# Zero products in PE's waits at the end of attention and in the first routing, a shorter list, and a later first step of the next routing

## The chip, the cores and the metric

One NeuronCore of a Trainium2 chip runs the whole program. Its engines work side by side: PE (TensorE) multiplies matrices, DVE (VectorE) and ACT (ScalarE) work on vectors, POOL (GpSimd) and SP (SyncE) mostly issue DMAs, POOL the ones that gather by an index. Each engine takes its instructions in the order in which the program wrote them and waits where an operand is not there. PE's clock has two levels, 1.2 and 2.4 GHz; the profile gives the granted clock of a stretch as a share of the higher one. The metric is the device time of one execution in microseconds (us); the time shown for a kernel is the median of its runs.

## What is computed

```python
scores = scale * np.matmul(q, k.transpose(0, 1, 3, 2))        # B, H, S, D = 4, 8, 576, 64
scores = np.where(masks[None], scores, -1e9)                  # a window, or a dilated window, by head
attn = np.exp(scores - max); attn /= attn.sum(-1) + 1e-9
x = np.matmul(attn, v)  ->  N = 2304 tokens of 512

logits = x @ w_gate                                           # E = 8 experts
for idx in np.argsort(-logits.flatten()):                     # greedy, largest logit first
    tok, e = idx // E, idx % E
    if assigned[tok] >= 0 or counts[e] >= N // E: continue    # cap = 288 tokens for each expert
    assigned[tok] = e; counts[e] += 1
x = for each e: relu(x[assigned == e] @ w1[e]) @ w2[e]        # F = 1024

P = exp(x @ w_gate2 - max), eight rounds of row and column scaling
out = sum over e of P[:, e] * (relu(x @ w1b[e]) @ w2b[e])     # every expert on every token
```

## The kernel before

**Attention** runs over NU = 25 units (a batch element, half of the heads, a block of rows). In the loop over n stand, for different units, the exponentials (ACT), the scores of the next unit (PE, L174 and L181), the transposes of the weights into the PSUM tile `ps_p` (`p_trans`, PE L207), their copy (`p_evac`, DVE or ACT), the product with V (`pv`, PE L228), the turn of its result (L270), and the logits of finished tokens (L300). Behind the loop stand the last turns and logits; a copy on DVE (L375) brings the logits to the router.

**The router** is written as a generator, `phase(ph)`, one phase for each expert. It finds the greedy choice not by sorting but expert by expert: the expert that fills up next is found by a search for its threshold, six steps (`STEPS`) of a few bits each. In a step DVE compares all tokens with the step's candidates (`G`, L504), PE counts with 18 small products (L576), DVE compares the counts with what is left (`ok`, L585), and PE adds up (`count`, L588), whose largest entry (`cur`, L590) starts the next step. Then comes the **list**: flags `ze`, two products with a matrix of ones and a triangular one (L618, L619), a scan and a few steps on DVE (L621 to L632) that give each token its place, two halves of a one-hot matrix (`G`, L640), 18 products (L671) that collect the token numbers, and `idx` (L676), by which POOL gathers the tokens (L877). `books()` (L654 to L660) brings mask and logits up to date, and a last product (L683) counts how much of each expert was used.

At each `yield` the generator hands out how much PE work, in ns, should lie between it and its next step. In phase 0 there is no such work; there `stage1` itself steps through it and puts two products of zeros (`warm(2)`, L808) where the number is over 2000. From phase 1 on `interleave` weaves the steps of the routing into the products of the expert found before:

```python
    room = 0.0
    for ns in main:
        room += ns
        while side is not None and room >= need:
            need = next(side, None)
```

`need` starts at 1900 and is then what the router hands out, times a factor.

**The first expert stage** (`main`) takes for each expert: the gathered tokens turned by PE (L922) and copied by ACT (`xt`, L923), the first layer (L907, ACT L912 and DVE L913 behind it), the second (L948), then the products of `m2_l1` and `m2_l2`, and `gate2` (L1283 to L1287), the logits of the second gate, whose last step is DVE's sum P (L1287). The weights w1a and w2a are gathered by POOL (L868) by the expert's number into four buffers `raw`, converted by ACT to a high half (L847) and by DVE to a low half (L838); `pump` calls these pieces at fixed places of the order, so DVE and ACT take them in the order of the program between the steps of the routing. The tiles `r` of the router have two PSUM buffers, shared with `gate2`.

**Stage 2** (L1176, L1214) runs every expert on every token and is the bulk of the time.

## Time and profile before

| | us |
|---|---|
| median of 3 runs | 1760.49 (1759.36 to 1765.73) |
| the profiled execution | 1749.37 |
| its span, first to last instruction | 1747.6 |
| PE busy | 1709.8 (98%) |
| DVE, ACT, POOL busy | 1341.5 (77%), 846.3 (48%), 238.6 (14%) |
| L1176 and L1214 in the chain that ended last | 27% and 25% |
| the routing of phase 0, from the first L576 to the first L907 | 111.87 to 145.08 |

PE is busy in 98% of the span. A busy PE is not a PE at its full clock: the granted clock is read for itself, by stretch. A row of a timeline gives the start, the duration, engine, line, operation, the tile written and those read, the count, and in brackets how long the engine was idle before and what released it. Durations of products contain a tail that overlaps the next one.

### The profile page before, as it was taken

Reading aid. Unit: us, or ns where it says so; the run is one execution under the profiler, and the core shown is the slowest. Engines: PE = TensorE matmul, PEld = TensorE weight load, DVE = VectorE, ACT = ScalarE, POOL = GpSimd, SP = SyncE. Lnnn points to the kernel's source line nnn. Section 1 sums busy time; section 2 is a strip of 40 time slices with the busy share of each in tenths; the row PEclk is TensorE's granted clock in tenths of the full one; section 3 lists DMA queues with packets and bytes.
Section 4 is the critical chain, followed back from the end, with each engine's and each line's share of the span. In section 5 each row is a group of like instructions: output and inputs, shape, how many; then the busy total and the mean of one; then the engine's idle time right before and its main releaser. Section 6 shows DMA issues by size and latency. Waiting matters only on the chain.

```text
span 1747.6 us, 34883 instructions
## 1 busy us (share of the span) xinstructions
PE 1709.8 (98%) x14326; PEld 1280.6 (73%) x14326; DVE 1341.5 (77%) x2572; ACT 846.3 (48%) x1544; POOL 238.6 (14%) x293
## 2 busy tenths in 40 slices
PE   9978999999999999999999999999999999999998
PEld 7956677767777577777777777777777777777777
DVE  6977777766647888878887887888788878886656
ACT  7833443334444455644445543565445544454433
POOL 1323333223410000000000000000000000000111
PEclk9977999999999999999999999999999999999999
DMA  9923444332733144343435235432544334433120
GB/s 330 279 59 110 124 125 134 95 98 77 213 99 102 76 163 154 137 159 112 176 127 209 88 138 211 155 130 89 201 161 157 123 131 155 165 138 148 37 100 37
DMA packets 107568, 241.19 MB, mean 138 GB/s; under 512 B 46384, under 2 KB 72496, under 8 KB 100496
## 3 DMA queue, kind: packets, MB, share of 16 engines
q1 hardware_dynamic: 86768, 151.64, 25.0%
q0 software_dynamic: 20384, 87.05, 14.3%
q8 instruction: 112, 1.84, 0.4%
q14 instruction: 48, 0.39, 0.1%
q10 hardware_dynamic: 256, 0.28, 0.1%
HBM read 173.64 MB, written 61.73 MB: 135 GB/s over the span
## 4 chain that ended last, share of the span: by engine, by line
PE 61%; issue 10%; DVE 5%; ACT 2%; POOL 1%; DMA 0%; POOLq 0%; ACTq 0%; DVEq 0%
PE mm L1176 27%; PE mm L1214 25%; PE mm L907 4%; PE mm L992 3%; PE mm L948 1%; DVE hl L1133 1%; POOL out_dram L1228 1%; ACT raw L1045 0%; DVE w1l L1048 0%; DVE r L1048 0%; DMA raw<-in_w2a_dram,widx 0%; DVE w2l L966 0%; PE r L576 0%; ACT hh L1132 0%; DVE xg L913 0%
## 5 line engine op out<-in xcount | busy, mean ns | idle before, releaser
L1176 PE MATMUL mm<-xb,w1h 128*128 128x384 f16 x2352 | 573.3, 326 | 1.3 <-DVE mm L1147 0.8
L1214 PE MATMUL mm<-w2h,hh 128*128 128x256 f16 x1764 | 480.8, 273 | 0.4 <-DVE t L1238 0.2
L1214 PE MATMUL mm<-w2l,hh 128*128 128x256 f16 x1764 | 480.8, 273 | 0.0
L1214 PE MATMUL mm<-w2h,hl 128*128 128x256 f16 x1764 | 480.8, 273 | 0.0
L1176 PE MATMUL mm<-xb,w1l 128*128 128x384 f16 x1176 | 383.3, 326 | 0.0
L1214 PEld LDWEIGHTS <-hh 128*128 128x128 f16 x3528 | 345.2, 98 | 43.0 <-issue 0.9
L1176 PEld LDWEIGHTS <-w1h 128*128 128x128 f16 x2352 | 230.0, 98 | 154.7 <-issue 6.6
L1214 PEld LDWEIGHTS <-hl 128*128 128x128 f16 x1764 | 172.6, 98 | 20.1
L1133 DVE TENSOR_TENSOR hl<-r,hh 128x1536 f16<-128x1536 f32 x84 | 147.5, 1756 | 41.2 <-ACT hh L1132 41.2
L1176 PEld LDWEIGHTS <-w1l 128*128 128x128 f16 x1176 | 115.0, 98 | 76.1
L1128 ACT ACTIVATE r<-mm 128x384 f32<-128x384 f32 x252 | 119.1, 481 | 100.5 <-PE mm L1176 100.5
L1094 POOL DMA_DIRECT2D ws<-raw x48 | 26.0, 541 | 928.6 <-ACT raw L1045 660.4
L1132 ACT ACTIVATE hh<-r 128x1536 f16<-128x1536 f32 x84 | 124.6, 1483 | 43.6 <-DVE r L1157 41.6
L1139 ACT ACTIVATE mm<-mm 128x384 f32<-128x384 f32 x84 | 40.3, 479 | 175.3 <-PE mm L1176 175.3
L1133 DVE TENSOR_TENSOR hl<-S,hh 128x1152 f16<-128x1152 f32 x84 | 113.5, 1351 | 0.0
L1224 DVE SCALAR_TENSOR_TENSOR acc<-t,P,acc 128x512 f32<-128x512 f32 x126 | 94.7, 752 | 4.5
L907 PE MATMUL mm<-xt,w1h 128*128 128x288 f16 x512 | 97.5, 290 | 0.0
L1132 ACT ACTIVATE hh<-S 128x1152 f16<-128x1152 f32 x84 | 96.4, 1147 | 0.4 <-DVE S L1161 0.4
L1045 ACT ACTIVATE raw<-raw 128x1024 f16<-128x1024 f32 x48 | 50.6, 1055 | 87.3 <-DVE raw L1029 45.8
L912 ACT ACTIVATE w1h<-mm 128x288 f16<-128x288 f32 (+1 forms) x120 | 46.9, 396 | 88.1 <-PE mm L907 87.9
L913 DVE SCALAR_TENSOR_TENSOR w1l<-mm,w1h 128x288 f16<-128x288 f32 (+1 forms) x120 | 50.0, 435 | 45.4 <-ACT w1h L912 45.3
L868 POOL DMA_INDIRECT raw<-in_w2a_dram,widx x64 | 75.9, 1186 | 55.3 <-issue 20.4
(265 smaller groups left out, 2921.5 us busy)
## 6 DMA issues: line engine op xcount, KB each, us to landing
xb<-xw SPq DMA_DIRECT2D x30, 1344.0 KB, 5.9
ws<-raw POOLq DMA_DIRECT2D x48, 448.0 KB, 3.3
ws<-r POOLq DMA_DIRECT2D x48, 448.0 KB, 3.0
raw<-in_w2b_dram SPq DMA_DIRECT2D x32, 512.0 KB, 4.4
raw<-in_w1b_dram SPq DMA_DIRECT2D x56, 256.0 KB, 9.0
w1h<-ws SPq DMA_DIRECT2D x6, 1792.0 KB
w1l<-ws SPq DMA_DIRECT2D x6, 1792.0 KB
w2h<-ws SPq DMA_DIRECT2D x6, 1792.0 KB, 7.2
```

What stands on the lines that cost most here:

```text
L868: self.nc.gpsimd.indirect_dma_start(out=r[:, i, :], out_offset=None, in_=rows[lay], in_offset=bass.IndirectOffsetOnAxis(ap=widx[:, c:c + 1 ...
L907: nc.tensor.matmul(p, a[:, k, 128 * f:128 * (f + 1)], rhs(k, b), start=(done[f] == 1 and i == 0), stop=(done[f] == KT and i == 2), skip_gr ...
L912: nc.scalar.activation(h[0][:, f, :n], p, AF.Relu)
L913: nc.vector.scalar_tensor_tensor(h[1][:, f, :n], p, 0.0, h[0][:, f, :n], op0=OP.max, op1=OP.subtract)
L992: nc.tensor.matmul(p, a[:, f, c], b[:, f, :], start=(f == 0 and n == 0), stop=(f == FT - 1 and n == 2))
L1045: self.nc.scalar.activation(hi[:, k], x, AF.Copy, scale=sw)
L1128: nc.scalar.activation(o, p, AF.Relu, scale=SH)
L1132: yield nc.scalar.activation(hq[0][:, i, k], x, AF.Copy)
L1133: yield V.tensor_sub(hq[1][:, i, k], x, hq[0][:, i, k])
L1176: nc.tensor.matmul(p, w[u][:, 2 * j + i // 2, k, 128 * (i % 2):128 * (i % 2 + 1)], x[:, v, r, j], start=(q in (1, 5) and j == 0 and n == 0 ...
L1214: nc.tensor.matmul(p, h[u][:, i, a, 128 * t:128 * (t + 1)], w[v][:, i, b, :], start=(q in (1, 7) and i == 0 and j == 0), stop=(q in (2, 3) ...
L1224: V.scalar_tensor_tensor(self.acc[:, r, :], x, self.P[:, r, e:e + 1], self.acc[:, r, :], op0=OP.mult, op1=OP.add)
```

## The change

It has six parts.

1. At the end of attention products of zeros are added on PE: `full` writes n of 128 columns to the unused end of a bank of the tile `ps_p` (12 ahead of the last scores but one, 18 between the last full unit's transposes and the next `pv`, 12 ahead of the turn of unit NU-2), and `busy` one of 512 columns behind each of the last logits and six at the end.
2. In phase 0 of the routing the zeros at each step are set by a table: 5 (for 2) ahead of each set of L576, 1 (for 0) ahead of each count, 6 (for 2) ahead of the list, 14 (for 2) ahead of L671; 24 (for 8) behind the list; and 2 behind the turns of each of the first two groups of tokens.
3. The list needs two steps less on DVE: the triangular matrix gets -1000 on its diagonal and the scan begins at 1000, so that a place of a token that isn't chosen is over 1000, and the smaller of two places replaces two products and a sum. `books` has one step more.
4. A small DMA `near` on POOL reads parts of the token array in phase 0 ahead of the gathers; the first gather then has fewer semaphores to wait for.
5. `interleave` begins with `need` 3300 for 1900. The first step that it places, the count of phase 1's first search step, then comes later among the first expert's products, and with it all steps behind it.
6. A second tile `z` of `ps_s` takes the zeros, and the last `ps_p` is allocated later.

```diff
+        def full(p, n):
+            for _ in range(n):
+                nc.tensor.matmul(p[:, 1, 4 * QB:], zero[:, :128], zero[:, :512 - 4 * QB], start=False, stop=False,
+                                 skip_group_check=True)
...
             if n < NU:
                 exps(n)
+            if n == NU - 3:
+                full(wide, 12)
             if n + 1 < NU:
                 scores(n + 1)
                 row_max(n + 1)
...
-                p_evac(n - 1, p_trans(n - 1))
+                wide = p_trans(n - 1)
+                if n == NU - 2:
+                    full(wide, 18)
+                p_evac(n - 1, wide)
...
-        last = [ps.tile([128, 2, 512], F32, name=name, bufs=1) for name in ("ps_v", "ps_p")]
+        last = [ps.tile([128, 2, 512], F32, name="ps_v", bufs=1)]
...
+        z = ps.tile([128, 2, 512], F32, name="ps_s")
+
+        def busy(n):
+            for _ in range(n):
+                nc.tensor.matmul(z[:, 0, :], zero[:, :128], zero, start=True, stop=True)
...
+        full(wide, 12)
         behind[-2]()
         x_turn(NU - 2, last[0])
         for n, c in enumerate(rest[:apart]):
             logits(o[:, n], c)
+            busy(1)
+        last.append(ps.tile([128, 2, 512], F32, name="ps_p", bufs=1))
         x_turn(NU - 1, last[1])
...
             logits(o[:, apart + n], c)
+            busy(1)
+        busy(6)
...
+FAR = 1000.0
...
-    f["tri"] = -(p[:, None] > p[None, :]).astype(np.float32)
+    f["tri"] = -(p[:, None] > p[None, :]).astype(np.float32) - FAR * np.eye(128, dtype=np.float32)
...
-        V.tensor_tensor_scan(out=pos, data0=self.one_f, data1=p[:, :2 * NC], initial=0.0, op0=OP.mult, op1=OP.add)
-        zv = wk.tile([128, 2 * NC], F32, name="zv")
+        V.tensor_tensor_scan(out=pos, data0=self.one_f, data1=p[:, :2 * NC], initial=FAR, op0=OP.mult, op1=OP.add)
         V.tensor_add(pos, pos, p[:, 64:64 + 2 * NC])
-        V.scalar_tensor_tensor(zv, pos, CAP + 0.5, ze, op0=OP.is_le, op1=OP.mult)
-        V.tensor_mul(pos, pos, zv)
         r = wk.tile([128, NC], F32, name="r")
-        V.tensor_add(r, pos[:, :NC], pos[:, NC:])
+        V.tensor_tensor(r, pos[:, :NC], pos[:, NC:], op=OP.min)
...
-            V.scalar_tensor_tensor(self.mask, zv[:, NC:], -100.0, self.mask, op0=OP.mult, op1=OP.add)
+            V.tensor_scalar(up, pos[:, NC:], CAP + 0.5, -100.0, op0=OP.is_le, op1=OP.mult)
+            V.tensor_add(self.mask, self.mask, up)
...
+IDLE = {4000: 5, 1900: 1, 2900: 5, 2400: 6, 6000: 14, 1200: 0}
...
+            if ph == 0 and g < 2:
+                self.warm(2)
             yield 640
...
-            if need > 2000:
-                self.warm(2)
+            self.warm(IDLE[need])
             if i in (2, 4):
                 late.pop(0)()
+            if i == 6:
+                near = self.xp.tile([38, 2], F16, name="near", bufs=1)
+                xd = self.xd
+                nc.gpsimd.dma_start(near, bass.AP(tensor=xd.tensor, offset=xd.offset + S * (B - 1) * 2 * DM,
+                                                  ap=[[30 * DM, 38], [DM, 2], [1, 1]]))
...
         next(first)
-        self.warm(8)
+        self.warm(24)
         next(side)
...
-        interleave(main(), side, lambda: SLACK if self.ph == 1 else SL2, need=1900)
+        interleave(main(), side, lambda: SLACK if self.ph == 1 else SL2, need=3300)
```

The order in PE's queue in one step of the first search (G the candidates' comparison, r the counts), before:

```order
L576 MATMUL r<-A,G 128x8
L588 LDWEIGHTS count
L588 MATMUL r<-ok,count 128x8
L808 LDWEIGHTS zero
L808 MATMUL mm<-zero 128x512
...
L576 LDWEIGHTS G
```

and in the changed kernel:

```order
L598 MATMUL r<-A,G 128x8
L831 LDWEIGHTS zero
L831 MATMUL mm<-zero 128x512
L610 LDWEIGHTS count
L610 MATMUL r<-ok,count 128x8
L831 LDWEIGHTS zero
L831 MATMUL mm<-zero 128x512
...
L598 LDWEIGHTS G
```

A zero product stands ahead of the count, and five instead of two behind it.

PE's queue where the first expert's first layer begins (xg gathered tokens, xt the turned ones), before:

```order
L922 LDWEIGHTS xg
L922 MATMUL mm<-id_102,xg 128x96
L588 LDWEIGHTS count
L588 MATMUL r<-ok,count 128x8
L808 LDWEIGHTS zero
L808 MATMUL mm<-zero 128x512
...
L907 LDWEIGHTS w1h
L907 MATMUL mm<-xt,w1h 128x288
```

and in the changed kernel:

```order
L945 LDWEIGHTS xg
L945 MATMUL mm<-id_102,xg 128x96
L831 LDWEIGHTS zero
L831 MATMUL mm<-zero 128x512
...
L930 LDWEIGHTS w1h
L930 MATMUL mm<-xt,w1h 128x288
```

The count of phase 1's first step has gone from here; it stands behind the first twelve products of the layer.

DVE's queue in the first layer (w2l the low half of a converted piece of w2a, w1l behind L913 that of the layer's result), before, from the second step's comparison on:

```order
L504 TENSOR_TENSOR G<-m,x 128x288 x2
L913 SCALAR_TENSOR_TENSOR w1l<-mm,w1h 128x288
L581 TENSOR_TENSOR base<-thr,x 128x32
L585 TENSOR_TENSOR ok<-r,rem 32x8
L838 SCALAR_TENSOR_TENSOR w2l<-raw,w2h 128x1024
L913 SCALAR_TENSOR_TENSOR w1l<-mm,w1h 128x288
L590 TENSOR_REDUCE cur<-r 128x1
...
L838 SCALAR_TENSOR_TENSOR w2l<-raw,w2h 128x1024
L581 TENSOR_TENSOR base<-thr,x 128x32
L585 TENSOR_TENSOR ok<-r,rem 32x8
L913 SCALAR_TENSOR_TENSOR w1l<-mm,w1h 128x288
L838 SCALAR_TENSOR_TENSOR w2l<-raw,w2h 128x1024 x2
```

and in the changed kernel:

```order
L526 TENSOR_TENSOR G<-m,x 128x288 x2
L936 SCALAR_TENSOR_TENSOR w1l<-mm,w1h 128x288
L861 SCALAR_TENSOR_TENSOR w2l<-raw,w2h 128x1024
L936 SCALAR_TENSOR_TENSOR w1l<-mm,w1h 128x288
L603 TENSOR_TENSOR base<-thr,x 128x32
L607 TENSOR_TENSOR ok<-r,rem 32x8
...
L861 SCALAR_TENSOR_TENSOR w2l<-raw,w2h 128x1024
L612 TENSOR_REDUCE cur<-r 128x1
...
L861 SCALAR_TENSOR_TENSOR w2l<-raw,w2h 128x1024 x2
L603 TENSOR_TENSOR base<-thr,x 128x32
L607 TENSOR_TENSOR ok<-r,rem 32x8
```

The second ok now stands behind the first w2l, the third behind all four.

## Rows read from the trace of the kernel before

**Rows 1.** The clock: mean granted TensorE clock and span of the core.

```profile
core 0: 1747.6 us, clock 0.988
```

**Rows 2.** By stretch: busy us of PE PEld DVE ACT POOL, PEclk, DMA.

```profile
108.40:116.40 8.00, 4.86 (x75) 3.02 (x72) 6.53 (x24) 0.83 (x3) 0.00 (x0) 0.50 0.09 25
...
143.80:149.40 5.60, 5.60 (x24) 3.19 (x24) 2.03 (x8) 1.47 (x2) 4.38 (x5) 0.51 0.54 150
149.40:161.60 12.20, 12.20 (x137) 9.39 (x136) 10.18 (x26) 5.53 (x9) 2.28 (x3) 1.00 0.31 86
```

**Rows 3.** PE's waits from 150 to 200 us: total, times, longest.

```profile
PE r L618 <- DVE ze L607: 1.2, 1, 1.2
PE r L576 <- DVE G L504: 1.0, 2, 0.7
PE r L671 <- DVE G L640: 0.6, 1, 0.6
PE mm L907 <- DVE x2l L953: 0.5, 1, 0.5
```

**Rows 4.** Line L683: PE idle before it, us and times, by releaser.

```profile
  DVE P L1287: 5.6, 5
```

**Rows 5.** PE's timeline, attention's end: start, duration, instruction [idle before, releaser].

```profile
93.05 0.38 PE L174 MATMUL ps_s<-mk 96*96 96x256 bf16 x2 [0.60 <-ACT e L200]
...
98.81 1.57 PE L228 MATMUL ps_v<-rawv,pt 128*96 128x65 f32 x16 [0.99 <-ACT x L244]
...
111.07 1.01 PE L808 MATMUL mm<-zero 128*128 128x512 f16 x2 [1.77 <-DVE L L375]
```

**Rows 6.** PE's timeline near the start: four zero products at full clock.

```profile
9.94 1.04 PE L161 MATMUL ps_v<-zero 128*128 128x512 f16 x4
```

**Rows 7.** PE's timeline, the search, and one set of L576 at full clock.

```profile
117.58 1.04 PE L576 MATMUL r<-A,G 128*128 128x8 f16 x18
118.86 0.16 PE L588 MATMUL r<-ok,count 32*128 32x8 bf16 x1 [0.24 <-DVE ok L585]
...
121.28 0.16 PE L588 MATMUL r<-ok,count 32*128 32x8 bf16 x1 [0.24 <-DVE ok L585]
...
149.36 0.77 PE L576 MATMUL r<-A,G 128*128 128x8 f16 x18
```

**Rows 8.** DVE's timeline, first list, and the third phase's chain to P.

```profile
129.24 0.20 DVE L624 SCALAR_TENSOR_TENSOR zv<-pos,ze 128x36 f32<-128x36 f32 x1
129.47 0.20 DVE L625 TENSOR_TENSOR pos<-pos,zv 128x36 f32<-128x36 f32 x1
...
221.49 0.17 DVE L590 TENSOR_REDUCE cur<-r 128x1 f32<-128x8 f32 x1 [2.17 <-PE r L588]
...
234.51 0.17 DVE L1287 TENSOR_TENSOR P<-r,P 128x16 f32<-128x16 f32 x1
```

**Rows 9.** PE's timeline, from the list to the first layer.

```profile
132.20 0.44 PE L671 MATMUL r<-rhs,G 128*128 128x6 f16 x9 [2.63 <-DVE rhs L647]
...
143.74 0.16 PE L588 MATMUL r<-ok,count 64*128 64x8 bf16 x1 [1.49 <-DVE ok L585]
...
145.08 0.69 PE L907 MATMUL mm<-xt,w1h 128*128 128x288 f16 x2
...
158.38 0.93 PE L576 MATMUL r<-A,G 128*128 128x8 f16 x18
```

**Rows 10.** ACT's timeline, conversions of weights and copies of xt.

```profile
139.21 1.06 ACT L847 ACTIVATE w1h<-raw 128x1024 f16<-128x1024 f32 x1 [1.30 <-DMA raw<-in_w1a_dram,widx]
140.64 2.46 ACT L923 ACTIVATE xt<-mm 128x768 f16<-128x768 f16 x3 [0.37 <-DMA oidx<-idx]
...
155.07 1.06 ACT L847 ACTIVATE w2h<-raw 128x1024 f16<-128x1024 f32 x1 [0.58 <-DMA raw<-in_w2a_dram,widx]
```

**Rows 11.** POOL's timeline, gathers of w2a, the first and the last.

```profile
140.48 1.70 POOL L868 DMA_INDIRECT raw<-in_w2a_dram,widx  x1 [2.21 <-DVE w1l L838]
...
151.28 1.01 POOL L868 DMA_INDIRECT raw<-in_w2a_dram,widx  x1 [0.30 <-issue]
```

More of the change, by code (lines that the diff above doesn't have):

```diff
@@ L804, in warm @@
     def warm(self, n, width=512):
+        if not n:
+            return
         p = self.psum()[:, :width]
@@ L1330, in stage1 @@
     def stage1(self, ctx, late):
+        nc = self.nc
         pool = lambda n, b: ctx.enter_context(self.tc.tile_pool(name=n, bufs=b, side="right"))
```

## The prediction

> **What bounds the kernel now.** I read the views in this order: the clock, the table by stretch, PE's waits, then the timelines of PE, DVE, ACT and POOL around the places that the diff touches. The profiled execution spans 1747.6 us [rows 1] and took 1749.4 us in all, so 1.8 us lie around the span; it is 11 us under the median of 1760.5. The sum below is made against 1749.4 and carried over to the median unchanged. A measurement of this kernel can tell about 0.5% from no change, 8.8 us; my chances go by that.
>
> PE is the bound nearly everywhere, and stage 2, over half of the time, is not touched. What the change can reach is small and lies in three places. First, the stretch from 108.4 to 149.4 us, in which PE ran at half clock (granted clock 0.50 and 0.51 of full, 1.2 GHz against 2.4) [rows 2]: the search for the first expert, its token list, the gathers and the entry to the first layer. Ahead of it PE had a few waits and tiny products; the clock came back after 5.6 us in which PE was busy without a gap, and stayed [rows 2]. Second, PE's 3.3 us of waits in the next phase [rows 3]. Third, five waits of 1.1 us, 5.6 us in all, before the product of L683, one in each later phase [rows 4]. Nothing else in PE's queue that the diff touches waits.
>
> **The end of attention.** Twelve zero products go ahead of the last scores but one, eighteen between the transposes of the weights and the product with V, twelve more ahead of the first of the last three turns. Four zeros of 512 columns took 1.04 us at full clock [rows 6], so one of 128 columns takes some 0.06. What the first twelve delay, 0.7 us, is taken up by the 0.60 us for which PE waited for ACT at 93.05; the third twelve and the products among the logits fall into waits that are there as well, and the last six into the 1.77 us before 111.07 [rows 5]. The eighteen, 1.1 us, have no cover: the product behind them feeds DVE, the next turn and ACT's copy, for which PE waits 0.99 us at 98.81 [rows 5], and so the end moves. I take **+1.05 us**; between +0.4 (if half is absorbed there) and +1.7 (both batches in full).
>
> Here a rule speaks against the change. The rows have a zero of 512 columns at 0.26 us with its tail, a quarter of which is what I use. The Trainium skill, "TensorE: Matmul & The Clock Gate", section "Back-to-back issue gap", says that in a real stream of a weight load and a product of 128 columns each pair takes about 81 ns, since the weight load is not hidden; every one of these zeros loads its weights anew. By that, an estimate from the page, the eighteen would cost 1.5 us and the sum would be 0.4 us worse. No run here shows such a stream, and the sum goes by the rows.
>
> **The search at full clock.** With zeros in all its waits PE is hardly idle from 105 us on, so I expect the clock to hold. One step takes 2.42 us from count to count; its 18 products take 1.04 us at half and 0.77 at full clock [rows 7], 0.27 less. The five zeros, 5 x 0.216 = 1.1 us, replace two at half clock, 1.04 us: no loss. The one more before the count lies in the wait for DVE's ok. Four or five of the six steps gain, one is bound by DVE: **-1.25 us** (0 to -1.6).
>
> **List and gathers.** DVE loses two of its steps between the scan and the index, one every 0.23 us [rows 8]: -0.46. The 14 zeros, 3.0 us, replace two at half clock and the wait of 2.63 us [rows 9], 3.65 together, less 0.46: covered. The products of L671 gain some 0.1 by the clock. **-0.6 us.** The small DMA `near` takes waits off the first gather of tokens; by the gap that it leaves that is worth 0 to 0.35 us on a path that does not bind here, so 0. Up to this point the index comes 0.8 us earlier.
>
> **The entry.** Before, the count of expert 1's first search step and three zeros stand ahead of the first layer, and PE waits 1.49 us for ok, which stands behind four conversions on DVE; the layer begins at 145.08 [rows 9]. Now twelve of its products stand ahead of that count. Next to bind is ACT: its fourth conversion of weights ends at 140.27, waiting for DMA, and three copies of xt take 2.46 [rows 10]; with 0.2 us less upstream the layer can begin at 142.7, 2.4 us earlier. Its first 18 products took 4.28 us at half clock (145.08 to 149.36) [rows 7, 9], half of that at full: 2.1 us more. So PE is 4.5 us ahead at 149.4.
>
> **Most of that is given back.** In the new DVE order the second ok stands behind the first w2l conversion and a w1l, and the third behind all four w2l; before, it stood ahead of the last two. These hang on the gathers of w2a: eight that start at 140.48, when DVE frees a buffer, run one after the other on POOL until 152.3 [rows 11], and ACT's last w2h waits for a DMA until 155.07 [rows 10]. They can come only about 0.6 us earlier (DVE's chain from the index, plus one more bookkeeping step, 0.2). PE reaches the second count at 148.5 and finds ok at 151.2: 2.8 us of waiting. It reaches the third at 155.7 and finds ok at about 157: 1.3 more. The same point of the layer lies at 157.65 in the trace of before (six products at 0.12 ahead of 158.38 [rows 9]). Left of 4.5: **-0.5 us** (this sum holds the three terms above and the +1.05). If the w2a gathers bind less, up to -4.5; if POOL comes no earlier, 0.
>
> **The later phases.** The other minimum, 3300 for 1900, puts the routing's steps 1.0 to 1.5 us of PE work later against the experts' products, in every phase. In the next phase the waits for ze, G and x2l, 3.3 us [rows 3], are reshuffled: PE asks later, and DVE has more behind it. The wait for ze should go, one of the others may grow: **-1.2 us** (+1 to -3.3). For L683 nine products of 256 columns more stand between the gate's products and it: 9 x 0.106 = 0.95 us (estimate from the products above). What it waits for is the end of a DVE chain that runs nearly without a gap from the last count at 221.49 to P's sum at 234.51 [rows 8]. That chain begins 1.1 to 1.4 us later, loses 0.46, gains 0.2, and some 0.5 of it now runs ahead of the count; so P comes 0.6 later and each wait shrinks by 0.4, five times: **-2.0 us** (0, if DVE moves as far as PE; -4.9, if DVE does not move). The bookkeeping's added step costs 0.2 us on DVE per phase; it is in this term.
>
> **Sum.** -0.5 - 1.2 - 2.0 = -3.7 us: 1745.7 by the profile, **1756.8** by the median.
>
> **The rivals.**
> - *The entry's gain is kept.* If the w2a pieces land 3 us earlier than I think, or ok(2) does not wait for them, the 4.5 us stay; with -2 in the next phase and -4 at L683 that is -10.5: 1750.0. For it: POOL's first gather took 1.70 us, the last 1.01 [rows 11], which could be contention that moves away. Against: the chain index, conversions, buffers, gathers is DVE's and POOL's, and the clock does nothing for these. Chance 0.22.
> - *New waits eat the rest.* The later steps of the routing meet other work on DVE; the waits at L683 stay at 1.1, those of the next phase stay at 3.3, and the entry gives back all. Then what is left is the cost of attention's zeros and one or two new waits of 0.5: +2, 1762.5. For it: the DVE chain ahead of L683 has hardly a gap [rows 8]. Chance 0.22.
> - *The clock falls all the same, and the zeros cost.* Place: from 108 to 143 us. A zero is 0.43 us at half clock; a step of the search is then 5 x 0.43 + 1.0 + 0.43 + 0.1 = 3.7 instead of 2.42 us, five times, +6; the 6 and the 14 ahead of list and gathers +3.2; the 24 run 10.3 us, longer than the tokens need, so that the first layer begins some 13 us late. It then runs at full clock and finds its weights, 2.3 back: +11, 1771.5. It decides only if half clock lasts through both search and list; if it lasts for a few microseconds, it is one step, +1. Against: 5.6 us without a gap brought the clock back [rows 2], and the stream of zeros has fewer gaps than that stretch's neighbours. Chance 0.06.
>
> **How the numbers follow.** Forecast 0.50, rivals 0.22, 0.22 and 0.06. The forecast's own bounds, entry 0 to -1.5, next phase +1 to -3.3, L683 0 to -4.9, make 1751 to 1762. The range leaves out the slow rival and the far half of the first: 1749 to 1766, its upper end being the second rival with another 3.5 us for the zeros of attention and a scatter of the median. Faster by over 0.5% (under 1751.7): most of the first rival, 0.22. Slower by over 0.5% (over 1769.3): 0.06. Within: 0.72.
>
> **What would show it.** Granted clock near 1.00 from 105 to 160 us; steps of 2.1 us in the search; the first layer beginning at about 142.7; PE waiting some 3 us for ok in its first third and then over 1 us more; waits at L683 (now at another line) of 0.6 to 0.8. Wrong, if PE does not wait there, if those waits stay at 1.1 or go altogether, or if half clock shows in the search.

## The result, and the profile after

The changed kernel took **1775.24 us** (median of six runs, 1773.53 to 1785.0) beside 1760.34 for the kernel before on the same chip: ratio **1.009, interval 1.0066 to 1.0114**, 15 us slower. The prediction was 1756.8 (1749 to 1766); it is wrong. The profiled execution took 1774.9 us.

The same kernel was measured three more times, each on another chip: 1.0017 [1.0003, 1.0032], 1.0021 [1.0012, 1.0031] and 1.0116 [1.0102, 1.0131]. So there are two things to explain: 3 to 4 us that are lost everywhere, where -3.7 was forecast, and 11 to 17 more that are lost on some chips.

Span and mean clock first (compare [rows 1]):

```profile
core 0: 1773.1 us, clock 0.989
```

Then the table by stretch (compare [rows 2]): time, length, busy time of PE, PEld, DVE, ACT and POOL with their counts, PE's clock, share of the DMAs, GB/s.

```profile
95.00:100.00 5.00, 5.00 (x74) 4.62 (x73) 3.55 (x7) 4.06 (x16) 2.44 (x4) 1.00 0.16 44
100.00:105.00 5.00, 3.70 (x38) 3.52 (x37) 1.99 (x5) 3.32 (x10) 2.98 (x4) 0.72 0.81 185
105.00:110.00 5.00, 5.00 (x53) 5.00 (x53) 1.59 (x5) 1.81 (x4) 2.33 (x4) 0.50 0.77 136
110.00:115.00 5.00, 5.00 (x55) 4.27 (x54) 3.52 (x13) 2.21 (x6) 0.38 (x1) 0.50 0.14 39
115.00:120.00 5.00, 5.00 (x80) 3.56 (x80) 2.63 (x10) 1.15 (x3) 0.00 (x0) 0.50 0.01 3
120.00:125.00 5.00, 4.93 (x32) 2.13 (x31) 1.84 (x8) 0.00 (x0) 0.00 (x0) 0.74 0.00 0
```

PE has no gap from 105 to 120 us, and yet runs at half clock there: the zeros fill its waits and the clock falls all the same. It fell at about 102 us, just behind a wait of PE for ACT, and came back between 122.5 and 123, behind the last zeros. Waits of PE from 95 to 200 us (us in total, times, longest):

```profile
PE r L610 <- DVE ok L607: 3.1, 1, 3.1
PE r L691 <- DVE G L659: 2.3, 2, 1.8
PE ps_v L233 <- ACT x L249: 1.3, 1, 1.3
```

The 3.1 us for `ok` stand where the prediction put a wait of 2.8, but only half of them has the cause that it gave. DVE's own row for this `ok` is

```profile
163.81 0.15 DVE L607 TENSOR_TENSOR ok<-r,rem 32x8 bf16<-32x8 f32 x1 [1.55 <-remote]
```

It was not held by the conversions ahead of it: DVE was idle for 1.55 us. "remote" means that the profile names no instruction of the core as the releaser. (On the chips of after_third and after_again, where no wait is "remote", PE waits 1.55 and 1.66 us here.) The wait for x, 0.99 before [rows 5], has grown to 1.3, and the clock fell just behind it. The product at the end of each phase, now L703 (compare [rows 4]):

```profile
  DVE P L1312: 2.2, 5
```

5.6 us have become 2.2. That much looks like a gain. Then the waits of all engines from 200 to 460 us show more of the "remote" ones, of which the trace of before has none:

```profile
DVE cur L612 <- remote: 15.5, 3, 5.6
ACT xt L946 <- remote: 13.8, 5, 5.6
...
PE r L598 <- DVE G L526: 5.0, 2, 2.5
```

The timeline of one of these places:

```profile
260.92 0.84 PE L945 MATMUL mm<-id,xg 96*128 96x96 f16 x16
...
261.70 0.17 PE L610 MATMUL r<-ok,count 32*128 32x8 bf16 x1
261.80 0.51 PE L945 MATMUL mm<-id,xg 96*128 96x96 f16 x8
...
265.79 1.51 ACT L946 ACTIVATE xt<-mm 128x768 f16<-128x768 f16 x2 [2.04 <-remote]
265.82 0.17 DVE L612 TENSOR_REDUCE cur<-r 128x1 f32<-128x8 f32 x1 [5.63 <-remote]
266.24 0.83 DVE L526 TENSOR_TENSOR G<-m,x 128x288 f16<-128x288 f32 x2
266.76 0.99 PE L598 MATMUL r<-A,G 128*128 128x8 f16 x18 [2.50 <-DVE G L526]
```

PE recorded the count at 261.70 and the turns at 261.80; ACT and DVE, whose operands these products are, go on 4 us later and within 0.03 us of each other, and then PE waits 2.5 us for DVE. The profile models the ends of products, so these rows don't tell whether the product was late or only the signal of it. On another chip (after_third) `cur` follows the same product within 0.21 us:

```profile
261.12 0.17 PE L610 MATMUL r<-ok,count 32*128 32x8 bf16 x1
...
261.33 0.17 DVE L612 TENSOR_REDUCE cur<-r 128x1 f32<-128x8 f32 x1 [1.26 <-PE r L610]
```

Laid side by side by the program's own events, the first trace is 17.3 us behind after_third at the start of stage 2: 3.9 arise up to the first set of counts of the search, where half clock lasted some ten microseconds longer, 1.9 up to the first expert's second layer (the 1.55 us of `ok` among them), 10.8 from the end of the third expert's routing to the sixth's, in these stalls, and the rest is small. Stage 2 adds another 2.1. The longer half clock is not a matter of that chip: the profiled run of a_need1900, on a chip without stalls, has it too, up to about 119.7 us.

### The profile page after: what moved, and what is told of

Read it like the earlier page. It is cut to its first block, busy times and chain, and to the rows that moved or that the text cites. A ratio compares the mean times of both kernels' runs of the same rounds, so it can differ in the third digit from the quotient of the medians.

```text
span 1773.1 us, 35106 instructions
## 1 busy us (share of the span) xinstructions
PE 1733.9 (98%) x14441; PEld 1295.4 (73%) x14441; DVE 1339.4 (76%) x2563; ACT 844.6 (48%) x1544; POOL 232.1 (13%) x294
## 4 chain that ended last, share of the span: by engine, by line
PE 74%; issue 11%; DVE 9%; ACT 2%; DMA 2%; POOL 2%; another core or an unknown queue 1%; SPq 0%; POOLq 0%; DVEq 0%; ACTq 0%
PE mm L1201 27%; PE mm L1239 25%; PE mm L930 7%; PE mm L1017 4%; PE mm L973 3%; PE ps_v L233 2%; PE ps_s L181 1%; PE r L598 1%; PE ps_p L207 1%; POOL out_dram L1253 1%; DVE hl L1158 1%; DMA raw<-in_w2a_dram,widx 1%; DVE G L659 1%; DVE w2l L991 1%
## 5 line engine op out<-in xcount | busy, mean ns | idle before, releaser
L930 PE MATMUL mm<-x2l,w0h 128*128 128x256 f16 x288 | 78.5, 272 | 0.9 <-DVE x2l L978 0.9
```

The costliest lines, as they stand in the source:

```text
L930: nc.tensor.matmul(p, a[:, k, 128 * f:128 * (f + 1)], rhs(k, b), start=(done[f] == 1 and i == 0), stop=(done[f] == KT and i == 2), skip_gr ...
```

## The experiments

The kernels after_fourth, b_att, b_near and c_best ran together on a chip that has those stalls, all others below on chips without. Ratios are to the kernel before on the same chip. What a kernel gains or loses between two events is the time between them in its trace set against the same time in the trace of before.

### The parts

The changed kernel again, and with need=1900:

```diff
-        interleave(main(), side, lambda: SLACK if self.ph == 1 else SL2, need=3300)
+        interleave(main(), side, lambda: SLACK if self.ph == 1 else SL2, need=1900)
```

> The changed kernel once more, beside its parts on one chip, where before took 1752 in the last runs. In its first trace 11 us went in phases 3 to 5, where DVE and ACT waited 4 to 6 us for products of PE (the counts and turns of the tokens) that PE's records show as done; with the same order neither the run with need=3300 alone nor the one without attention's zeros has that. Theory 1 (these stalls belong to this program): they are here again, some 1767 to 1770, 15 to 18 over before. Theory 2 (they belonged to that chip or its runs): none here, 1759 to 1762, as with need=1900.

> The changed kernel with need=1900 again, all zeros and the shorter list kept. In the changed kernel's trace, against before, the end of attention and the first search are 8.8 us later (2.2 us more came in at the start, in a wait for the first load), the entry and the next phase near nothing, phases 3 to 5 10 us, stage 2 2.5 us. Theory 1 (the order costs): the later first step puts a count between the turns of the tokens in each phase, and that is the 10 us; this run takes 1764 to 1767 and has no wait of 2.5 us for G. Theory 2 (the zeros cost, and what is seen later follows from them): no change, 1773 to 1777.

after_again: 1756.31 us, 1.0017 [1.0003, 1.0032]. a_need1900: 1759.97 us, 1.0044 [1.0028, 1.0061], from four runs; a second measurement below gave 1.0019. So undoing need=3300 does not mend the kernel on such a chip.

The other direction, need=3300 alone in the kernel before:

> The kernel before with need=3300 alone. Theory 1: 9 to 12 us slower than before, 1769 to 1772, with waits of 2.5 us for G of L504 in phases 3 to 5 and a count (L588) in the middle of the turns (L922). Theory 2: as before, 1760, or 2 to 5 us faster by shorter waits at L683.

1754.08 us, 1.0008 [0.9997, 1.0018]: no difference that can be measured. Yet the waits at L683 have gone down just as in the changed kernel, and the waits of PE from 200 to 455 us say where it went:

```profile
PE r L683 <- DVE P L1287: 2.2, 5, 0.4
PE mm L907 <- DVE x2l L953: 2.1, 5, 0.4
```

Ahead of each shorter wait for P stands a new one for `x2l`, the same DVE chain at an earlier point. From the end of the third phase to the end of the seventh this kernel gains 0.20 us, and the kernel before, run again, 0.27: the 3.4 us of shorter waits are worth nothing.

Now the zeros: the changed kernel without those at the end of attention (a_noatt: the calls of `full` and `busy` left out), without any added zeros (a_nozeros: also `warm(2)` for the table, 8 for 24), without `busy` alone (a_nobusy), without `full` alone (a_nofull), and without attention's zeros at need=1900 (a_noatt_1900). The lines left out, for a_noatt first, then those that a_nozeros changes besides:

```diff
-                full(wide, 12)
...
-                    full(wide, 18)
...
-        full(wide, 12)
...
-            busy(1)
...
-            busy(1)
-        busy(6)
...
-            if ph == 0 and g < 2:
-                self.warm(2)
...
-            self.warm(IDLE[need])
+            if need > 2000:
+                self.warm(2)
...
-        self.warm(24)
+        self.warm(8)
```

> The changed kernel without the zeros in attention (full and busy), those of the first routing and need=3300 kept. Theory 1: the attention zeros' 1.7 us of PE work and the earlier fall of the clock they bring cost 6 to 9 us, so 1766 to 1769; the later phases stay as in the changed kernel. Theory 2: all of the zeros' cost lies in attention and what follows, 1760 to 1763. If the fall of the clock has another cause than these zeros: 1772 to 1775.

> The changed kernel with no zeros in attention and those of before in the first routing (2 at the steps over 2000, 8 behind the list, none among the turns); need=3300, the shorter list and near kept. Theory 1: 1768 to 1771, the order's cost alone, less 1 us for the list. Theory 2: 1757 to 1761.

> The changed kernel without the zeros among the last logits and the six behind them (busy), the 42 of 128 columns (full) kept. Theory 1 (busy is the cost: three of them stand ahead of the last turn, on which DVE's last chain waits, and thirteen take 0.43 us each at half clock): 5 to 6 us less than the changed kernel on the same chip, and the first set of counts 4 to 5 us earlier. Theory 2 (full is the cost): 1 to 2 us less.

> The changed kernel without the 42 zeros of 128 columns (full), busy kept. Theory 1: 1.5 to 2.5 us less than the changed kernel. Theory 2: 4 to 6 us less.

> The changed kernel without any zeros in attention and with need=1900: what is left are the zeros of the first routing, the shorter list and near. Theory 1: the zeros bring the clock back before the entry and the list is 0.5 us shorter, while the later first step gives 2 us in the later phases and loses 3.5 in the entry: 1750 to 1752, 0 to 2 us under before and 1 to 2 under the run with need=3300. Theory 2 (the zeros of the first routing cost as much as they bring): 1753 to 1755.

| | median us | ratio | interval | clock, profiled run |
|---|---|---|---|---|
| after_again | 1756.31 | 1.0017 | 1.0003 to 1.0032 | 0.994 |
| a_nobusy | 1757.42 | 1.002 | 1.0005 to 1.0035 | 0.991 |
| a_nofull | 1754.6 | 1.0008 | 0.9995 to 1.0021 | 0.993 |
| a_noatt | 1753.62 | 0.9998 | 0.9987 to 1.0008 | 0.993 |
| a_nozeros | 1753.01 | 1.0003 | 0.9994 to 1.0013 | 0.983 |
| a_noatt_1900 | 1752.84 | 1.0003 | 0.999 to 1.0016 | 0.993 |

Without attention's zeros the ratio is 0.9998 or 1.0003, with all of them 1.0017 to 1.0044 on such chips: some 3 us. This compares ratios of different chips, since a_noatt and the whole kernel did not run together; on the chip that had both after_again and a_noatt_1900 the two intervals overlap. That `busy` alone is the cost fell: without it the kernel is not faster. The zeros of the routing do what they are for, the clock goes from 0.983 to 0.993, and buy no time that can be measured.

### What attention's zeros do

The zeros of attention alone, in the kernel before (with the tile `z` and the later `ps_p` that go with them):

```diff
+            if n == NU - 3:
+                full(wide, 12)
...
+                if n == NU - 2:
+                    full(wide, 18)
...
+        full(wide, 12)
...
+            busy(1)
...
+            busy(1)
+        busy(6)
```

> The kernel before with the zeros at the end of attention alone. Theory: the zeros cost by themselves, about 1 us for the eighteen and 1 to 2 us for the others, which stand ahead of DVE's last chain: +2 to +3.5 us, ratio 1.0012 to 1.002; in the profile the first set of candidates begins 20 us (late fall of the clock) or 23 us (early fall) after the last unit's scores, where the kernel before has 18.8 and 21.3. Rival: they only matter together with the five zeros ahead of the first search step, whose first one is at half clock, and cost 1 us or less here, 1.0006.

1772.2 us (median of five runs; a sixth, of 7285 us, is not in the ratio), **1.0033 [1.002, 1.0046]** on a chip where the kernel before takes 1767.76: 4.4 us by the medians, 5.8 by the ratio. Its clock fell late, at 110.7 us, as in the trace of before and in spite of the wait of 1.30 us for x, and still the first set of counts comes 4.3 us later, measured from the last unit's scores. PE's and DVE's rows there:

```profile
95.50 1.17 PE L212 MATMUL ps_p<-zero 128*128 128x128 f16 x18
100.66 1.57 PE L233 MATMUL ps_v<-rawv,pt 128*96 128x65 f32 x16 [1.30 <-ACT x L249]
...
112.95 3.15 PE L378 MATMUL ps_s<-zero 128*128 128x512 f16 x7
...
114.69 0.62 DVE L525 TENSOR_TENSOR G<-m,thr 128x448 f16<-128x448 f32 x1
...
116.16 1.01 PE L829 MATMUL mm<-zero 128*128 128x512 f16 x2
```

This has two parts. DVE's last `G` ends 21.4 us behind the scores, 19.7 in the trace of before: +1.7, the eighteen and what else lies on the way to DVE's chain. And PE gets to the first counts only at 117.0, 1.7 us after that G; before, it had begun them 0.9 us ahead of its end. That is the seven zeros at half clock, 3.15 us, with two more behind them: the wait of 1.77 us that I had taken for their cover [rows 5] was too short, since at half clock the zeros are twice as long and outlast it.

The kernel before, unchanged, beside its own other runs:

> The kernel before, nothing altered: it gives the scatter of one kernel against itself and a profile from the same chip as the others of this call. Both theories: 1.000 within 0.001; the end of attention (scores of the last unit to the first set of candidates) 18.8 us if the clock falls late as in the first profile, about 21 us if it falls early, within 10 us of the last scores, as it did in every changed kernel. If the chip of this job is one on which products are seen late by DVE and ACT (theory A on a bad chip), this trace shows such stalls too.

1753.67 us, 1.001 [0.9999, 1.002], so 0.1% is what one kernel differs from itself. Its profiled run is 4 us above that of the prediction, and its table by stretch says why:

```profile
100.00:105.00 5.00, 4.01 (x43) 3.87 (x42) 2.30 (x6) 2.82 (x9) 3.45 (x4) 0.75 0.70 167
105.00:110.00 5.00, 4.92 (x51) 4.77 (x51) 2.12 (x10) 2.01 (x5) 2.23 (x3) 0.50 0.87 187
```

Here the clock falls at 102.5 us and not at 108.5 [rows 2], and the stretch from the last scores to the first counts takes 21.3 us for 18.8. The kernel before has both courses. Its timed runs on the four chips without stalls, sorted by their granted clock (one more run, at 0.983, took 1753.8):

| granted clock | runs | median us |
|---|---|---|
| 0.984 | 5 | 1757.4 |
| 0.985 | 18 | 1753.9 |
| 0.986 | 19 | 1752.4 |
| 0.987 | 25 | 1752.6 |
| 0.988 | 29 | 1751.0 |
| 0.989 | 12 | 1749.7 |

The changed kernel is sorted in the same way: 1757.9 at 0.992 (three runs), 1756.5 at 0.994 (five), 1753.4 at 0.997 (two), 1751.9 at 0.998 (one). (These are parts of its list, which runs from 0.991 to 0.998.) The two traces put the early fall at 2.5 us in the kernel before; that it is worth as much in the changed kernel is argued from the sorted times, since no profile shows its runs with the most clock. Twelve profiled runs of the changed kernel and of kernels made from it lost the clock between 100 and 104 us, with attention's zeros or without, c_best at 107; the zeros don't prevent it.

The second trace of before settles what attention's zeros do in the changed kernel, for in after_third the clock fell as early. The last turn (L275, before L270) and DVE's last G, with the zeros between them, of after_third and then of before_again:

```profile
114.92 0.33 PE L275 MATMUL ps_p<-idf,xg 96*128 96x96 f32 x2
...
116.94 1.67 PE L378 MATMUL ps_s<-zero 128*128 128x512 f16 x7
118.67 1.24 PE L831 MATMUL mm<-zero 128*128 128x512 f16 x5
...
119.38 0.62 DVE L526 TENSOR_TENSOR G<-m,thr 128x448 f16<-128x448 f32 x1
```

```profile
112.28 0.58 PE L270 MATMUL ps_p<-idf,xg 96*128 96x96 f32 x2
...
116.99 0.62 DVE L504 TENSOR_TENSOR G<-m,thr 128x448 f16<-128x448 f32 x1
```

From the last unit's first scores (95.19 and 95.37) the turn starts at 19.7 us, not 16.9, and G ends at 24.8, not 22.2. So it is the first of the two parts that counts here, 2.6 us on DVE's chain. The last zeros are covered: the clock is full again from 112.7 us, the seven take 1.67, and behind the five that follow the first counts begin 0.3 us before G ends. What has no cover stands ahead of the last turn. I had set the third twelve and the zeros among the logits against waits of PE in the trace of before, which lists, from 93 to 112 us,

```profile
PE ps_v L270 <- DVE L L302: 0.6, 1, 0.6
PE ps_s L300 <- DMA xT<-xd: 0.5, 2, 0.4
```

In before_again neither is there: at half clock PE has no wait from 101.1 to 114 us. The waits belonged to the course of the clock that the first trace happened to have.

### Entry and list

The shorter list alone, in the kernel before:

```diff
-        V.scalar_tensor_tensor(zv, pos, CAP + 0.5, ze, op0=OP.is_le, op1=OP.mult)
-        V.tensor_mul(pos, pos, zv)
...
-        V.tensor_add(r, pos[:, :NC], pos[:, NC:])
+        V.tensor_tensor(r, pos[:, :NC], pos[:, NC:], op=OP.min)
...
+            V.tensor_add(self.mask, self.mask, up)
```

> The kernel before with the shorter list alone (scan from 1000, smaller of two places, one more step in the bookkeeping). Theory: two steps of DVE of 0.23 us less in each of seven phases, but only phase 0 has nothing beside them: -0.46 us there, and at the five waits of the later phases (1.1 us each) 0.26 each (0.46 less, 0.2 more of bookkeeping), -1.3: together -1.8 us, ratio 0.999. Rival: the later waits keep their length because the other steps of DVE fill in, -0.5 us, 0.9997. Both are near what five rounds can tell; the lengths of the waits in the profile tell them apart (0.85 or 1.1 us).

1749.38 us, 0.9989 [0.9978, 1.0001], the fastest of all. The source view of the product at the phases' end (L682 here) has 0.9 for 1.1 each:

```profile
  DVE P L1286: 4.5, 5
```

From the end of the third phase to the end of the seventh it gains 1.38 us, 0.27 of which the kernel before shows too. In phase 0, where I expected 0.46, it gains nothing at the tokens, and POOL's timeline shows why:

```profile
133.14 1.20 POOL L867 DMA_INDIRECT raw<-in_w1a_dram,widx  x1 [25.20 <-DVE widx L616]
134.64 1.63 POOL L867 DMA_INDIRECT raw<-in_w1a_dram,widx  x1 [0.30 <-DVE md L630]
...
139.22 0.93 POOL L876 DMA_INDIRECT xg<-xd,idx  x1 [0.30 <-ACT w1h L846]
```

Four gathers of weights stand ahead of the first gather of tokens, without a gap. In the trace of before the second took less and POOL was idle ahead of the tokens:

```profile
130.35 0.95 POOL L868 DMA_INDIRECT raw<-in_w1a_dram,widx  x1 [0.30 <-DVE g L630]
...
134.90 0.93 POOL L877 DMA_INDIRECT xg<-xd,idx  x1 [0.98 <-ACT w1h L847]
```

There the tokens' gather goes out 0.9 us behind the end of DVE's `idx`, in b_list 1.5 behind it: the 0.6 us by which the index comes earlier are lost in POOL's queue. The second gather takes 1.6 to 1.7 us in all kernels with the shorter list but a_nozeros, and 0.95 in all without it; why is not shown.

Keeping the old order in phase 1 and moving the later phases:

```diff
-                    yield ns
+                    yield ns - 1400 * (ph == 1 and i == 0)
```

> The changed kernel without the attention zeros, with need=1900 for the first interleaved step, and 1400 ns more of the expert's work ahead of the next routing step once, at the beginning of the second expert's first layer. So the first phase keeps its old order and the later phases get the later order that shortened their last wait. Theory: the entry's 2.1 us at full clock are kept as in the run with need=1900 and no attention zeros (1.0003), and the later phases give 1.0 to 1.5 us back as with need=3300: 0.9995 of the kernel before, -1 us, with the five waits ahead of the count of the used at 0.4 instead of 1.1 us. Rival: what the waits lose comes back at the next counts in full, 1.0003 as before.

1753.37 us, 1.0007 [0.9999, 1.0016]. The waits at the phases' end are 0.4 each, as wanted, and the kernel gains 1.19 us over the four later phases where a_noatt_1900, with waits of 0.9, gains 1.42. The rival held: what the wait loses comes back elsewhere.

The small DMA alone in the kernel before, and a version from all that was learned (no zeros in attention, need=1900, no `near`, two zeros for five ahead of the first search step):

```diff
+            if i == 6:
+                near = self.xp.tile([38, 2], F16, name="near", bufs=1)
...
-IDLE = {4000: 5, 1900: 1, 2900: 5, 2400: 6, 6000: 14, 1200: 0}
+IDLE = {4000: 2, 1900: 1, 2900: 5, 2400: 6, 6000: 14, 1200: 0}
```

> The kernel before with the small DMA near alone. Theory: near (its tile, or its place in the queue) is what makes PE wait for the last expert's weights near 507 us, 1.4 to 1.6 us, so that this run has waits for ACT w1h or DVE w1l there and is 1 to 1.6 us slower, 1.0006 to 1.001. Rival: those waits come from the shift of the stage-2 weight loads against the gathers of w2a (by the earlier or later course of the phases ahead), and near does nothing: 1.000, no such waits.

> The changed kernel without attention's zeros, with need=1900, without near, and with two zeros instead of five ahead of the first search step. Theory: the run without attention's zeros and with need=1900 was 1.0003; the first step's three zeros at half clock are worth 1.3 us and near 1.6, so 0.9985 to 0.999, -2 to -2.6 us, the fastest of all. Rival: the clock then comes up one step of the search later or not before the list, the search's gain goes (0.9 us) and the waits for the last weights stay: 1.000.

b_near 1769.13 us, 1.0001 [0.9991, 1.0011]; c_best 1766.65 us, 0.9996 [0.9986, 1.0006], both beside 1767.76. `near` makes no difference that can be measured, as the prediction had it. None of the waits for w1h and w1l shows here, but the whole changed kernel has none on this chip either (after_fourth), so b_near can't tell what brings them. On chips without stalls every kernel made from the changed one has one or both of them, and none made from the one before; after_third, from 462 to 610 us:

```profile
PE mm L1017 <- ACT w1h L935: 1.0, 1, 1.0
...
PE mm L1017 <- DVE w1l L936: 0.7, 1, 0.7
```

Between two products on either side of them, near 503 and 506 us of the trace of before, after_third loses 2.1 us, after_again 1.8, a_noatt_1900 1.9 and a_nozeros 0.9; before_again, b_list and b_need3300 lose nothing. That is nearly as much as the end of attention costs, and the prediction has no term for it. ACT's copy stands behind a conversion of w2a that waits for its DMA; what makes that DMA late stays open. No version clearly beats the kernel before by more than the 0.1% by which it differs from itself; b_list comes nearest, with an interval that just includes no change.

### The stalls

> The changed kernel, nothing altered, beside the kernel before on the same chip. So far it was 1.009 of the kernel before in one job and 1.0017 in another; the trace of the first shows 10.9 us lost in the third to fifth routing phase, in stalls of 4 to 6 us in which DVE and ACT wait for products that PE's records show as done, the trace of the second none of them. Theory A: those stalls belong to the first job's chip and not to the edits; then the ratio here is 1.001 to 1.004 (+2 to +7 us) and the waits view names no such stall of DVE or ACT. Theory B: the changed program has two courses, and the slow one comes back; then 1.007 to 1.011 with the stalls in the same phases.

> The changed kernel, nothing altered, on whichever chip this job gets. If the stalls of 4 to 6 us in the third to fifth routing phase belong to the chip of the first job, the ratio is 1.001 to 1.003 and the waits view shows none of them, as twice before. If they are a second course of the program, they come in some jobs: 1.007 to 1.011.

after_third: 1755.83 us, 1.0021 [1.0012, 1.0031], no such stall. after_fourth, on the chip of b_att, b_near and c_best: 1787.7 us beside 1767.76, **1.0116 [1.0102, 1.0131]**, and the stalls are back. Waits of all engines from 200 to 460 us, of after_fourth and then of b_near:

```profile
DVE cur L612 <- remote: 21.5, 4, 5.7
ACT xt L946 <- remote: 21.1, 7, 5.6
...
PE r L598 <- DVE G L526: 8.2, 3, 2.8
```

```profile
ACT x2h L952 <- remote: 10.9, 5, 2.2
DVE ok L585 <- remote: 2.4, 1, 2.4
```

The kernel before itself is 15 us slower on this chip (1767.8 against 1752) and has such stalls as well, at other places: in b_near, which differs from it by a DMA that moves no time, ACT waits 2.2 us at `x2h` in each of five phases and in the last phase at `xt`. c_best has a single one of 2.3 us between 200 and 460 us, at `ok`, and 6.6 us at `xt` in the last phase. So the stalls come with the chip, or with the session on it, which these runs can't tell apart; where they fall goes with the order of the instructions. In the changed kernel a count and the turns of the next expert's tokens stand side by side (L610 between sixteen and eight products of L945 in the rows above), and both readers are held; DVE's next step hangs on the count, and PE on that. That need=3300 is what brings them together is argued from this order and from c_best and b_near, which have 1900. Two runs were to test it:

> The kernel before with need=3300 alone, once more. Theory: need=3300 puts the count of a search step and the turns of the next expert's tokens side by side, and on a chip on which ACT and DVE see products late this falls on the path: on such a chip the ratio is 1.006 to 1.01 and the waits view shows cur and xt waiting 4 to 6 us between 250 and 440 us. On a chip without such delays 1.0008 as before, no such waits. Rival: the stalls need the other edits; then about 1.001 on any chip.

> The changed kernel with need=1900, once more. Theory: on a chip with late products it has the stalls of the kernel before (2.2 us at x2h in each phase, more in the last phase) and none of 4 to 6 us at cur, and takes 1.002 to 1.004, the price of attention's zeros; on a chip without them 1.001 to 1.004 (it was 1.0044 in four runs). Rival: the stalls at cur and xt are there with need=1900 too, 1.009 or more.

They met a chip without stalls: 1751.91 us, 0.9999 [0.9985, 1.0013], and 1756.51 us, 1.0019 [1.0001, 1.0037], no "remote" waits. They repeat the price of the parts, and the question of need=3300 on the other kind of chip stays open, as does what holds ACT and DVE back.

## Why the prediction was wrong

Two things have to be kept apart: the time that came out, and the sum behind it. On chips without stalls the ratio was 1.0017 to 1.0021, which on the median of 1760.5 is some 1764 us, within the range, though the way was the other one: slower, not faster. What carried the time out of the range were the stalls of the first chip.

The sum can be checked step by step against traces without stalls. The table gives, for after_third and after_again, what each step added or saved against before_again, whose clock fell as early; all are aligned at the last unit's scores.

| step | predicted | after_third | after_again |
|---|---|---|---|
| end of attention, up to the first counts | +1.05 | +3.2 | +3.2 |
| search, up to the list | -1.25 | -0.9 | -0.9 |
| list, up to the last product of the phase | -0.6 | -0.6 | -0.6 |
| entry, up to the first layer | -1.6 | -0.6 | -0.8 |
| first layer, up to the second | +1.9 | +0.9 | +0.9 |
| next phase, up to the second expert's second layer | -1.2 | -1.2 | +0.1 |
| later phases, up to the last expert's tokens | -2.0 | -1.2 | -1.3 |
| the last expert, up to stage 2 | 0 | +2.1 | +1.8 |
| sum | -3.7 | +1.6 | +2.4 |

- **The end of attention, +1.05 taken, +0.4 to +1.7 as bounds: measured +3.2** up to the first counts (24.6 us from the last scores, 21.3 in before_again), +2.5 up to the first `count`, and +2.6 on DVE's last G. This is the step that failed first. One part was right: eighteen zeros took 1.17 us with their tail, 1.1 expected. The Trainium skill, "TensorE: Matmul & The Clock Gate", section "Back-to-back issue gap", gives 81 ns for such a pair, which makes 1.5 us by estimate; the trace is below it. What was wrong is the cover. I set the other zeros against waits of PE that only the trace with the late fall of the clock has, and not against the moment at which DVE has the next operands, and I priced them at full clock: those ahead of the last turn push DVE's chain. The five zeros ahead of the first search step, which I took for no loss, are none in after_third; they are one where the clock is still half (a_noatt: 2.3 us for the five, the first `count` 1.2 us later than in before_again).
- **The clock from 105 us on, expected to hold: it fell** in every profiled run of the changed kernel and of those made from it; in the first trace it stayed down with PE busy from 105 to 120 us without a gap. My rival for it, at 0.06, was right about the fall, and wrong on its place and length: half clock lasted 10 us in after_again and 20 in the first trace, ahead of the search, and search and list ran at full clock. I had argued that "5.6 us without a gap brought the clock back" [rows 2]; in the first trace 15 us without a gap did not.
- **The search, -1.25: -0.9,** but not by the clock. 0.7 of it is the first set of products, which begins late and then doesn't wait for DVE's second G. The five steps behind it gain 0.04 us each: at full clock a step takes 2.38 us where I expected 2.1. The profile of after:

```profile
127.39 0.16 PE L610 MATMUL r<-ok,count 32*128 32x8 bf16 x1
127.49 1.25 PE L831 MATMUL mm<-zero 128*128 128x512 f16 x5
128.58 0.95 PE L598 MATMUL r<-A,G 128*128 128x8 f16 x18
129.39 0.38 PE L831 MATMUL mm<-zero 128*128 128x512 f16 x1
129.78 0.16 PE L610 MATMUL r<-ok,count 32*128 32x8 bf16 x1
```

  The eighteen products take 0.95, not 0.77: they begin at 128.58, and DVE has its second G at 128.85. The zero ahead of the count costs nothing, for the count goes out 0.06 us behind the end of `ok` in both kernels. The step hangs on DVE's chain at either clock (2.42 us at half).
- **List and gathers, -0.6: -0.6** up to the last product of the phase, right, and not handed on.
- **The entry, -1.6** (2.4 earlier in all, of which 0.8 came from the steps above): **-0.6 and -0.8.** PE no longer waits for `ok` there, and ACT's copies bind, as predicted: in after_third the layer begins 0.05 us behind the last of them. But they end 10.1 us behind the phase's last product, and 8.75 in the trace of before. The tokens' gather goes out 0.7 later against that product, as in b_list, and PE waits another 1.1 us for the data. I had ACT's conversions as the next bound and took them to come 0.2 earlier.
- **The first layer, +1.9: +0.9.** The waits for `ok` were predicted as 2.8 and 1.3 and are 1.55 and 0.84 in after_third: right in place and mechanism (DVE makes these `ok` directly behind the w1l and w2l named), 2.4 us in all for 4.1. In the first trace the 3.1 us look like the 2.8, but half of them are the stall: that agreement is luck. With the old order and full clock (a_noatt_1900) the layer takes 2.1 us less than in the trace of before, the 2.1 of the prediction; need=3300 then costs more than the clock gives.
- **The next phase, -1.2: -1.2 in one trace and +0.1 in the other.** The wait for ze, 1.2 us, is gone, and that for G grew from 0.6 to 1.8, as the prediction had it. What makes the two traces differ is not shown.
- **The waits at the phases' end, -2.0:** they shrank by 0.7 each, more than the 0.4 expected, and need=3300 gave nothing for it. The list gave the 1.2 to 1.3 us: b_list gains as much over these phases, b_need3300 nothing. The sign came out, for another reason than the main one given.
- **The last expert** is in no term of the sum. What it loses, with the waits for w1h and w1l, is more than the later phases gain.

Against before_again stage 2 thus starts 1.6 us later in after_third and 2.4 in after_again, in place of the -3.7 of the sum. The runs of before have a median some 1.5 us under that profile; that about half of them keep the clock longer is read off their granted clocks. Together this makes the 3.0 to 3.7 us that were measured.

The other 11 us of the official result are, as far as the traces tell, the stalls and a longer half clock; no trace of before exists from that chip, so what its own stalls cost there is not known. The one trace of before, taken where there were none, could not show them; but its time lay 11 us under the median of the runs, and I carried the sum over "unchanged". That was the second step that failed: the gap was a cost that the runs had and the trace had not, and a change of order could move it.

## What to carry to other kernels

A filler has no cover in a wait as such: compare the moment at which the filler ends, at the clock that it will really have, with the moment at which the next operand is ready. Take the waits from more than one execution: here 1.2 us of waits were there in one trace of the same kernel and not in another, in which the clock fell earlier. A shorter wait is a gain only if the next wait on the same chain does not grow; look ahead of it and behind it before counting it. And where the profiled execution lies well under the median of the runs, ask first what the others have that it does not.

## What the runs showed of the hardware

- PE, busy in 5.00 of 5.00 us in each of three stretches in a row, stayed at the lower clock level (granted 0.50) while it ran turns, products of 8 columns and single zeros between them. It rose between 122.5 and 123 us, behind seven zeros of 512 columns in a row. In after_third it rose between 112 and 113 us, behind twelve zeros of 128 columns and turns; the same zeros and turns, at 111.3 to 113.4 us of the first trace, were not followed by a rise.
- Twelve zeros of 128 columns with their weight loads took 0.83 us at full clock and 1.48 at half, with their tails.
- In two of six sessions, each on one chip, ACT and DVE stood idle for up to 5.7 us ahead of operations on products that PE had recorded (4 us before, in the place shown), at the same places of several phases; in the other four never. The kernel before takes 1760 to 1768 us in the former and 1751 to 1752 in the latter. What holds them is not known.
